# Splitting the first weight load of a decode-attention kernel into 16 and 112 partitions, and moving the small input behind it

## The chip, the cores and the metric

The kernel runs on one core of a Trainium2 chip. The metric is device time in microseconds (us) per execution. The kernel before took 187.73 us at the median of the runs made beside the changed kernel, with a spread of under 0.2 us.

## The reference, cut to what matters

One decode step of attention with grouped heads: 32 sequences, 32 query heads, 8 key/value heads of width 128, a window of the last 512 positions of each cache.

```python
q = (x @ wq)                        # (32, 512) @ (512, 4096)
k, v = k_cache[:, :, -512:], v_cache[:, :, -512:]
p = softmax(q @ k.T * 128 ** -0.5)
out = (p @ v) @ wo                  # (32, 4096) @ (4096, 512)
```

The two windows are 33.5 MB each, `wq` and `wo` 4.2 MB each: 75.5 MB must be read once.

## The kernel before

Everything is written in Bass with explicit semaphores. SP (SyncE) issues nearly all loads on one queue, in a fixed order, and waits only for a buffer to come free. The parts that matter here:

```python
w_sb = sb("w_sb", [P, DKT, HD], BF16)        # 128 partitions x 32 KB
...
nc.scalar.dma_start(x_sb, x.rearrange("b s d -> b (s d)")).then_inc(sem_x, 16)   # 32 KB, ACT's queue
wq_rows = wq.rearrange("(p t) n -> p (t n)", t=DKT)
wq_half = DKT * HD // 2
nc.sync.dma_start(                            # first half of wq: 128 rows of 16 KB
    w_sb[:, 0:2, :].rearrange("p k n -> p (k n)"), wq_rows[:, 0:wq_half]
).then_inc(sem_wq[0], 16)
...
# SP: the second half of wq, then K and V blocks of 2 MB each, then wo
sp.dma_start(w_sb[:, 2:4, :]..., wq_rows[:, wq_half:]).then_inc(sem_wq[1], 16)
for name in DMA_ORDER: ...
...
# TensorE: transpose x, then q = x @ wq in two halves
pe.wait_ge(sem_x, 16)
...
for kt in range(DKT):
    if kt % 2 == 0:
        pe.wait_ge(sem_wq[kt // 2], 16)
    for k in range(2):
        for c in range(4):
            ins = pe.matmul(X_ps[32 * c:32 * c + 32, k, :], lhsT=xT_sb[:, kt, :], rhs=w_sb[:, kt, ...], ...)
```

Each load of this kernel adds 16 to its semaphore, in 16 steps of one that the trace shows one by one; I call these steps its marks. The packet records show sixteen packets of 4 bytes at the end of each load, some 0.4 us before its marks (7.52 to 7.95 us for the first half of `wq`, its marks 7.92 to 8.32), so I read each mark as the end of a sixteenth of the load. Between 4 and 170 us, 15 to 17 packets of 16 KB were under way 99% of the time. "Engine" below means one of the 16 DMA engines that the profile's page counts; the records do not name the engine of a packet or of a mark, so what is said of single engines is read from the order in time.

## Time and profile before

| | before |
|---|---|
| median time, us | 187.73 |
| span of the profiled run, us | 185.9 |
| first packet of the stream / last mark of the last load, us | 1.81 / 182.90 |
| marks of the first half of wq, first to last, us | 7.92 to 8.32 |
| marks of the second half of wq, us | 12.81 to 13.22 |
| mean time of one 16 KB packet in steady flow (packets 33 to 128), us | 0.611 |

The span is measured from the first to the last recorded instruction of the core; the median time is some 1.8 us longer. The profile's page gives busy shares, and its DMA row the share of 40 slices in which the 16 DMA engines were at work. The trace also holds every DMA packet (start, length, bytes) and every semaphore mark. The lines themselves are in the prediction below, which reads them.

### The profile page before, as it was taken

What the parts mean: (1) busy time and instruction counts of PE and PEld (TensorE: products, weight loads), DVE (VectorE), ACT (ScalarE), POOL (GpSimd) and SP (SyncE); (2) the same over time, 40 slices, a digit from 0 to 9 for tenths busy, and PEclk for the clock granted to TensorE, in tenths of its full rate; (3) what the DMA queues carried; (4) which work ended last, traced back from release to release, by engine and by line L of the source; (5) the groups of instructions that cost most, each with busy time, mean ns of one, the idle gap of its engine ahead of it and who ended that gap; (6) DMA issues with size and microseconds to landing.
All of it is one profiled execution on the core that took longest, in us unless ns stands there. A gap on an engine that the chain in (4) does not pass through costs nothing.

```text
span 185.9 us, 3841 instructions
## 1 busy us (share of the span) xinstructions
PE 110.3 (59%) x1604; PEld 90.7 (49%) x1604; DVE 131.8 (71%) x239; ACT 82.4 (44%) x142; POOL 32.1 (17%) x82
## 2 busy tenths in 40 slices
PE   0232004346179925949726992459699975999851
PEld 0100001032069804929326881129669974999741
DVE  0006999689999799985899959999999993010001
ACT  3001000259420199011992039826989999711011
POOL 7100390500700071050420060000030000000000
PEclk9999999999999995796955899657999999699999
DMA  6999999999999999999999999999999999999980
GB/s 208 419 444 423 430 430 419 444 423 426 426 419 430 426 419 430 434 419 434 418 430 430 423 434 412 441 430 416 432 416 430 423 430 426 423 430 404 401 326 25
DMA packets 6160, 75.80 MB, mean 408 GB/s; under 512 B 704, under 2 KB 768, under 8 KB 1792
## 3 DMA queue, kind: packets, MB, share of 16 engines
q1 hardware_dynamic: 6096, 75.53, 96.2%
q8 instruction: 12, 0.20, 0.4%
q10 hardware_dynamic: 48, 0.03, 0.1%
q14 instruction: 4, 0.03, 0.0%
HBM read 75.53 MB, written 0.03 MB: 406 GB/s over the span
## 4 chain that ended last, share of the span: by engine, by line
DMA 58%; DVE 22%; PE 11%; issue 4%; SPq 3%; ACT 0%; DVEq 0%
DMA V_sb<-in_v_cache_dram 31%; DVE KT_sb L426 14%; DMA w_sb<-in_wo_dram 12%; DMA K_sb<-in_k_cache_dram 8%; PE O_ps L353 7%; DMA w_sb<-in_wq_dram 6%; DVE w_sb L448 4%; DVE QA_sb L416 2%; PE S_ps L316 2%; SPq L211 2%; PE X_ps L296 1%; PE PT_ps L335 1%; SPq L200 1%; DVE oT_sb L409 0%; DVE KT_sb L404 0%
## 5 line engine op out<-in xcount | busy, mean ns | idle before, releaser
L426 DVE STREAM_TRANSPOSE KT_sb<-K_sb 128x2048 uint32<-128x2048 uint32 x32 | 72.3, 2287 | 1.2 <-DMA K_sb<-in_k_cache_dram 1.1
L353 PE MATMUL O_ps<-w_sb,V_sb 128*128 128x128 bf16 x640 | 46.1, 241 | 10.5 <-DMA V_sb<-in_v_cache_dram 5.6
L353 PEld LDWEIGHTS O_ps<-w_sb,V_sb 128*128 128x128 bf16 x640 | 44.7, 109 | 13.7 <-issue 7.0
L265 POOL COPY QBD<-QA_sb 32x64 bf16<-32x64 bf16 x64 | 25.6, 540 | 79.6 <-PE S_ps L316 62.0
L515 ACT ACTIVATE w_sb<-PTc,mask 128x512 bf16<-128x512 bf16 x60 | 38.9, 729 | 0.0
L316 PE MATMUL S_ps<-KT_sb,QBD 128*32 128x512 bf16 x256 | 20.9, 479 | 26.3 <-DVE KT_sb L426 19.8
L448 DVE TENSOR_SCALAR w_sb<-PTc,mask 128x512 bf16<-128x512 bf16 x100 | 30.2, 370 | 4.9 <-PE O_ps L353 4.9
L316 PEld LDWEIGHTS S_ps<-KT_sb,QBD 128*32 128x32 bf16 x256 | 7.8, 110 | 35.9 <-issue 32.0
L487 ACT ACTIVATE X_ps<-S_ps,negmax 128x512 f32<-128x512 f32 x8 | 5.3, 659 | 42.2 <-DVE negmax L435 42.2
L335 PE MATMUL PT_ps<-P_bf,pick 128*128 128x128 bf16 x128 | 11.8, 265 | 18.0 <-ACT P_bf L496 14.7
L335 PEld LDWEIGHTS PT_ps<-P_bf,pick 128*128 128x128 bf16 x128 | 10.2, 122 | 20.9 <-ACT P_bf L496 16.3
L525 ACT ACTIVATE oT_sb<-O_ps 128x128 bf16<-128x128 f32 x8 | 6.0, 750 | 26.0 <-PE O_ps L353 26.0
L515 ACT ACTIVATE K_sb<-PTc,mask 128x512 bf16<-128x512 bf16 x24 | 15.3, 717 | 1.6 <-DVE KT_sb L426 1.6
L353 PE MATMUL O_ps<-K_sb,V_sb 128*128 128x128 bf16 x256 | 15.1, 217 | 1.3 <-DMA V_sb<-in_v_cache_dram 1.0
L353 PEld LDWEIGHTS O_ps<-K_sb,V_sb 128*128 128x128 bf16 x256 | 14.5, 96 | 2.1 <-issue 1.3
L448 DVE TENSOR_SCALAR K_sb<-PTc,mask 128x512 bf16<-128x512 bf16 x40 | 12.1, 377 | 0.3 <-ACT PTc L506 0.2
L353 PE MATMUL O_ps<-KT_sb,V_sb 128*128 128x128 bf16 x128 | 9.1, 240 | 2.4 <-DMA V_sb<-in_v_cache_dram 2.4
L353 PEld LDWEIGHTS O_ps<-KT_sb,V_sb 128*128 128x128 bf16 x128 | 8.9, 108 | 2.5 <-issue 2.5
L469 DVE CAST K_sb<-S_ps 128x256 bf16<-128x256 f32 x1 | 0.4, 424 | 12.7 <-PE S_ps L365 12.7
L515 ACT ACTIVATE KT_sb<-PTc,mask 128x512 bf16<-128x512 bf16 x12 | 7.8, 725 | 0.0
L467 DVE CAST K_sb<-X_ps 128x384 bf16<-128x384 f32 x1 | 0.6, 558 | 9.8 <-PE X_ps L365 9.8
L496 ACT ACTIVATE P_bf<-X_ps,recip 128x512 bf16<-128x512 f32 x8 | 5.5, 685 | 4.4 <-DVE recip L441 4.4
(41 smaller groups left out, 49.5 us busy)
## 6 DMA issues: line engine op xcount, KB each, us to landing
K_sb<-in_k_cache_dram SPq DMA_DIRECT2D x16, 2048.0 KB, 15.2
V_sb<-in_v_cache_dram SPq DMA_DIRECT2D x16, 2048.0 KB, 17.0
w_sb<-in_wq_dram SPq DMA_DIRECT2D x2, 2048.0 KB, 9.7
w_sb<-in_wo_dram SPq DMA_DIRECT2D x8, 512.0 KB, 20.3
oT_sb<-in_x_dram ACTq DMA_DIRECT2D x1, 32.0 KB, 4.5
out_dram<-oT_sb SPq DMA_DIRECT2D x1, 32.0 KB, 1.5
```

The lines of the kernel that those rows point to most:

```text
L211: sp.dma_start(wo_sb[:, hg].rearrange("p i n -> p (i n)"), wo[hg * 512:(hg + 1) * 512, :].rearrange("(m i) n -> m (i n)", i=4),).then_inc( ...
L265: pool.tensor_copy(dst[:, i, :, x0:x0 + 4], src).then_inc(pool_qbd, 1)
L316: ins = pe.matmul(S_ps[32 * c:32 * c + 32, q % 2, :], lhsT=QBD[:, q % 2, g, b, e, :], rhs=bass.AP(tensor=KT_sb, offset=s0 * slot + (b * G ...
L335: ins = pe.matmul(PT_ps[:, r, :], lhsT=pick[:, r, KS - s:KS - s + P], rhs=P_bf[:, s, :], start=(s == 0), stop=(s == KS - 1), tile_position ...
L353: ins = pe.matmul(O_ps[:, q % 2, 0:P], lhsT=V_sb[:, m % NV, r, :], rhs=z_of(q)[:, :, x0 + r, :], start=(e == 0 and r == 0), stop=(e == 1 a ...
L416: dve.tensor_copy(QA[32 * a:32 * a + 32, c], QW[32 * c:32 * c + 32, :, :, a::4].rearrange("p h k q -> p h q k"),).then_inc(dve_q, 1)
L426: dve.transpose(KT_w[:, n % NK, b].rearrange("p i r s -> p r i s"), K_w[:, n % NK, :, 32 * b:32 * b + 32],).then_inc(dve_T, 1)
L448: ins = dve.tensor_scalar(z_of(q)[:, k].rearrange("p x r -> p (x r)"), PTc[:, q % RING].rearrange("p x r -> p (x r)"), mask[:, k:k + 1], N ...
L487: act.activation(P_f32, S_ps[:, q % 2, :], ACTF.Exp, bias=negmax[:, q:q + 1], scale=SCALE, accum_out=sums[:, q:q + 1],).then_inc(act_exp, 1)
L496: act.activation(P_bf[:, :, :], P_f32.rearrange("p (x s) -> p s x", s=KS), ACTF.Copy, scale=recip[:, q:q + 1],).then_inc(act_P, 1)
L515: ins = act.activation(z_of(q)[:, k].rearrange("p x r -> p (x r)"), PTc[:, q % RING].rearrange("p x r -> p (x r)"), ACTF.Copy, scale=mask[ ...
L525: act.activation(oT_sb[:, :, 4 * q:4 * q + 4].rearrange("p h a -> p a h"), O_ps[:, q % 2, 0:P].rearrange("p (a h) -> p a h", a=4), ACTF.Co ...
```

## The change

The intent, as I read it: the first load is cut so that its first piece has sixteen rows, as many as there are packets under way at a time, in the hope that all of them start at once; and `x` leaves ACT's queue, where its packets (2.64 to 4.91 us) come between those of the first load.

```diff
-        nc.scalar.dma_start(x_sb, x.rearrange("b s d -> b (s d)")).then_inc(sem_x, 16)
         wq_rows = wq.rearrange("(p t) n -> p (t n)", t=DKT)
         wq_half = DKT * HD // 2
-        nc.sync.dma_start(
-            w_sb[:, 0:2, :].rearrange("p k n -> p (k n)"), wq_rows[:, 0:wq_half]
-        ).then_inc(sem_wq[0], 16)
+        for p0, p1 in ((0, 16), (16, P)):
+            nc.sync.dma_start(
+                w_sb[p0:p1, 0:2, :].rearrange("p k n -> p (k n)"), wq_rows[p0:p1, 0:wq_half]
+            ).then_inc(sem_wq[0], 16)
+        nc.sync.dma_start(x_sb, x.rearrange("b s d -> b (s d)")).then_inc(sem_x, 16)
...
-                    pe.wait_ge(sem_wq[kt // 2], 16)
+                    pe.wait_ge(sem_wq[kt // 2], 32 - 8 * kt)
```

The number of bytes, and the order of all compute instructions on every engine, stay as they were.

## The prediction

Passages that rest on things which no trace or run of this case shows are cut from the prediction, and from the expectations further down; the cuts are marked. One of them takes a term out of the forecast's sum. The sum came to +1.5 us, so 189.2 us, from three terms: -0.2 (an earlier start) and -0.07 (`x`), and the cost of the 16-row load. Of the rivals, the first is that the 16 rows cost no more than their bytes (given a third). Two more are given an eighth and a quarter; the second of these was that the 112 rows cost more than their bytes too. In the list of signs, those before its second cut belong to a slow 16-row load, those after it to one that costs its bytes alone.

> **What bounds the kernel now.** I read the page first (span, busy shares, DMA row, chain), then the landing times of the loads, then fine windows over the two ends of the run, then the packet records of the first microseconds. From the page:
>
> ```profile
> span 185.9 us, 3841 instructions
> PE 110.3 (59%) x1604; PEld 90.7 (49%) x1604; DVE 131.8 (71%) x239; ACT 82.4 (44%) x142; POOL 32.1 (17%) x82
> DMA  6999999999999999999999999999999999999980
> GB/s 208 419 444 423 430 430 419 444 423 426 426 419 430 426 419 430 434 419 434 418 430 430 423 434 412 441 430 416 432 416 430 423 430 426 423 430 404 401 326 25
> ...
> q1 hardware_dynamic: 6096, 75.53, 96.2%
> ...
> DMA 58%; DVE 22%; PE 11%; issue 4%; SPq 3%; ACT 0%; DVEq 0%
> ```
>
> No compute engine is above 71%, while the DMA row is full in every slice except the first and the last two, at some 425 GB/s. 75.53 MB at that rate are 178 us of the 185.9. So the kernel is one stream of loads with a start and a tail. The landing records say the same more sharply: the first of the 16 completion marks of each 2 MB load follows that of the load before by 4.88 to 4.98 us from beginning to end, so the earliest of the 16 DMA engines never runs dry. A compute wait in the middle costs nothing; a microsecond at the head of the stream comes out at the end. Windows of the start (window, length, the five engines, clock, DMA share, GB/s):
>
> ```profile
> 0.00:1.75 1.75, 0.00 (x0) 0.00 (x0) 0.00 (x0) 0.51 (x1) 0.92 (x8) 1.00 0.00 0
> 1.75:4.00 2.25, 0.00 (x0) 0.00 (x0) 0.00 (x0) 0.98 (x2) 2.10 (x3) 1.00 0.91 288
> 4.00:8.00 4.00, 0.28 (x4) 0.21 (x4) 0.29 (x1) 0.00 (x0) 1.43 (x7) 1.00 1.02 436
> ```
>
> Nothing moves before 1.75; the next 2.25 us run at 288 GB/s instead of 436, a loss of 2.25 x (1 - 288/436) = 0.76 us. That is all a better head could recover beyond the start itself. The timeline gives the issues, and the chain the tail:
>
> ```profile
> 0.80 0.41 ACTq L156 DMA_DIRECT2D oT_sb<-in_x_dram  x1
> ...
> 0.80 0.39 SPq L159 DMA_DIRECT2D w_sb<-in_wq_dram  x1
> ...
> 1.24 0.42 SPq L192 DMA_DIRECT2D w_sb<-in_wq_dram  x1
> ```
>
> ```profile
> 159.94 22.96 DMA w_sb<-in_wo_dram
> 182.90 0.04 issue
> 182.94 0.44 PE X_ps L388 x16
> ```
>
> The last wo mark at 182.90 starts a fixed tail of 3.0 us. The 16 marks of that load spread over 3.27 us (179.63 to 182.90) where those of the first load spread over 0.41, so the slowest engine sets the end.
>
> **The head, packet by packet.** The first packets (16 KB rows) start one engine after another from 1.81 to 2.41, one or two later still: a mean start near 2.08. They take 0.78 to 1.42 us, about 1.07, against 0.611 in steady flow. Packets of x, on ACT's queue, come in between from 2.64 on; five of them take 0.18 to 0.36 us instead of 0.045. The final store[...], starts its engines within some 0.12 us (184.91 to about 185.03). [...] The change aims at this.
>
> [...]
>
> **The change part by part.** (1) The first 2 MB load becomes 256 KB for partitions 0 to 15 and 1.75 MB for the rest. Bytes are unchanged; one more issue on SP costs about 0.4 us there, hidden because each 2 MB keeps the queue busy for 4.9 us. The second issue is at about 1.24, and its first rows should be ready near 2.25 (1.24 plus the 1.01 us between issue and first packet, 0.80 to 1.81), while the first row is in flight. Gain: the stagger mean goes from 0.27 to perhaps 0.05, so -0.2 us. (2) x leaves ACT's queue: its five slow packets cost about 1.2 us over 16 engines, -0.07 us each; its 32 KB still pass. x lands behind the first wq half instead of at 5.27. Transpose and evacuation take about 0.6 us and the first half's matmuls 1.9 us, but the second half lands 4.9 us after the first: 2.4 us of slack. The chain through q starts at the second half as before, so this costs nothing. [...] I put the number slightly lower, at 189.0, because the rivals below pull further down than up in weight.
>
> **The rivals.** [...] Then only -0.2 to -0.6 remains, counting that the first packet may also start 0.1 to 0.15 us earlier: the final store's first packet came 0.85 us after its issue began, the first load's 1.01. Time 187.1 to 187.5. For it: the change was evidently meant so, and 0.76 us is there to be had. [...] *It is hidden* fails on the full DMA row: there is no slack for a delayed head to vanish in. *A new wait on x* would need more than the 2.4 us of slack. One disturbance stays: twelve instruction-fetch packets of about 1.05 us fall on single engines in mid-run[...].
>
> **Range and chances.** 187.1[...] to 191.0[...] should hold it 8 times in 10. Two per cent are 3.75 us: a gain like that is impossible when only 1.81 us come before the first packet and 0.76 us are lost after it[...]. Faster 0.01, same 0.91, slower 0.08.
>
> **What would show each step.** [...] a low rate in the window 1.75 to 4, the last mark of the second wq half past 14.3 instead of 13.22, and all later landings shifted alike. [...] sixteen first packets starting within 0.1 us, taking about 1.1 us, and the second wq half landing near 12.8. [...] If x matters, the wait before the second wq half's matmuls ends on something other than the load. The prediction is wrong if the second wq half lands earlier than before, or if the head is delayed and the end is not.

## The result, and the profile after

| | before | after |
|---|---|---|
| median time, us | 187.73 | 191.15 |
| all runs, us | 187.68 to 187.83 | 190.72 to 191.47 |
| ratio | | 1.0178 (1.0161 to 1.0195) |
| span of the profiled run, us | 185.9 | 189.0 |
| last mark of the first half of wq, us | 8.32 | 11.58 |
| last mark of the second half of wq, us | 13.22 | 16.43 |
| last mark of the last load (wo), us | 182.90 | 185.96 |

The changed kernel is 3.42 us slower by the medians: within 2%, and 0.15 us above the stated range.

From the page of the changed kernel (span; DMA busy tenths and GB/s in 40 slices; the chain that ended last, by engine):

```profile
span 189.0 us, 3842 instructions
...
DMA  6999999999999999999999999999999999999980
GB/s 118 319 347 440 423 416 437 433 413 433 437 421 411 437 433 420 426 426 423 430 428 430 420 430 433 430 420 426 428 416 426 433 423 420 433 426 401 407 340 24
...
DMA 55%; DVE 25%; PE 11%; SPq 4%; issue 4%; DVEq 0%
```

The busy row is the same digit for digit, but the first three slices moved 118, 319 and 347 GB/s instead of 208, 419 and 444; from the fourth slice on the two rows are alike to some 5%. So the engines were occupied all the time and moved less. The busy share alone would have hidden it.

Windows of the head of the changed kernel (window, length, busy time of the five engines, clock, DMA share, GB/s). A packet counts, whole, in the window in which it starts, so a share can pass 1:

```profile
1.75:4.00 2.25, 0.00 (x0) 0.00 (x0) 0.00 (x0) 0.54 (x2) 2.10 (x3) 1.00 1.28 233
4.00:8.00 4.00, 0.00 (x0) 0.00 (x0) 0.00 (x0) 0.00 (x0) 1.43 (x7) 1.00 0.88 262
8.00:12.00 4.00, 0.10 (x4) 0.13 (x4) 0.00 (x0) 0.00 (x0) 0.00 (x0) 1.00 1.01 307
```

Before, the first two of these windows had 288 and 436 GB/s, and the third this line:

```profile
8.00:12.00 4.00, 1.90 (x16) 0.54 (x16) 0.00 (x0) 0.00 (x0) 0.00 (x0) 1.00 1.01 434
```

In time at 430 GB/s, 2.25 x (288 - 233) / 430 = 0.29 us are lost in the first window, 4 x (436 - 262) / 430 = 1.62 in the second and 4 x (434 - 307) / 430 = 1.18 in the third: 3.09 us, the whole difference of the spans. Most of it is lost after 4 us, that is, while the 112-row load runs.

The issues in the timeline, and the DMA list (KB each, us from issue to landing), of the changed kernel:

```profile
0.80 0.84 SPq L159 DMA_DIRECT2D w_sb<-in_wq_dram  x2
...
1.70 0.42 SPq L162 DMA_DIRECT2D oT_sb<-in_x_dram  x1
...
2.15 0.42 SPq L193 DMA_DIRECT2D w_sb<-in_wq_dram  x1
```

```profile
w_sb<-in_wq_dram SPq DMA_DIRECT2D x1, 2048.0 KB, 14.3
w_sb<-in_wq_dram SPq DMA_DIRECT2D x1, 1792.0 KB, 10.3
w_sb<-in_wq_dram SPq DMA_DIRECT2D x1, 256.0 KB, 4.2
oT_sb<-in_x_dram SPq DMA_DIRECT2D x1, 32.0 KB, 10.1
```

The issues are done by 2.57 us and were never late. But 256 KB took 4.2 us from issue to landing; before, a load eight times as large landed 7.5 us after its issue. The packet records show the rest: the sixteen rows of the small load start between 1.82 and 2.48 us and take 0.71 to 1.75 us; the next sixteen packets, the first of the 112-row load, take 1.59 us at the mean, and the later ones 0.75 to 1.09 us instead of 0.611.

The tail is unmoved: 185.96 to 189.0 after, 182.90 to 185.9 before, 3.0 us in both.

```profile
164.60 21.36 DMA w_sb<-in_wo_dram
185.96 0.04 issue
186.01 0.44 PE X_ps L389 x16
```

### The profile page after: what moved, and what is told of

The parts are those of the page before. It is cut to its first block, busy times and chain, and to the rows that moved or that the text cites. A ratio compares the mean times of both kernels' runs of the same rounds, so it can differ in the third digit from the quotient of the medians.

```text
span 189.0 us, 3842 instructions
## 1 busy us (share of the span) xinstructions
PE 108.9 (58%) x1604; PEld 89.5 (47%) x1604; DVE 131.7 (70%) x239; ACT 82.3 (44%) x142; POOL 32.0 (17%) x82
## 4 chain that ended last, share of the span: by engine, by line
DMA 55%; DVE 25%; PE 11%; SPq 4%; issue 4%; DVEq 0%
DMA V_sb<-in_v_cache_dram 30%; DVE KT_sb L427 15%; DMA w_sb<-in_wo_dram 11%; DMA w_sb<-in_wq_dram 8%; PE O_ps L354 7%; DMA K_sb<-in_k_cache_dram 6%; DVE w_sb L449 6%; SPq L212 2%; DVE QA_sb L417 2%; PE S_ps L317 2%; PE X_ps L297 1%; DVE maxv L434 1%; SPq L201 1%; SPq L159 0%; DVE oT_sb L410 0%
## 5 line engine op out<-in xcount | busy, mean ns | idle before, releaser
L354 PE MATMUL O_ps<-w_sb,V_sb 128*128 128x128 bf16 x640 | 46.9, 244 | 9.8 <-DVE w_sb L449 5.0
L354 PEld LDWEIGHTS O_ps<-w_sb,V_sb 128*128 128x128 bf16 x640 | 45.5, 111 | 12.5 <-DVE w_sb L449 6.5
L516 ACT ACTIVATE K_sb<-PTc,mask 128x512 bf16<-128x512 bf16 x24 | 15.3, 721 | 1.6 <-DVE KT_sb L427 1.6
L354 PE MATMUL O_ps<-KT_sb,V_sb 128*128 128x128 bf16 x128 | 7.5, 217 | 2.0 <-DMA V_sb<-in_v_cache_dram 2.0
L354 PEld LDWEIGHTS O_ps<-KT_sb,V_sb 128*128 128x128 bf16 x128 | 7.3, 96 | 2.1 <-issue 2.1
L482 ACT ACTIVATE KT_sb<-X_ps 128x512 bf16<-128x512 f32 x1 | 0.6, 597 | 16.1 <-PE X_ps L297 16.1
```

What stands on the lines that cost most here:

```text
L354: ins = pe.matmul(O_ps[:, q % 2, 0:P], lhsT=V_sb[:, m % NV, r, :], rhs=z_of(q)[:, :, x0 + r, :], start=(e == 0 and r == 0), stop=(e == 1 a ...
L516: ins = act.activation(z_of(q)[:, k].rearrange("p x r -> p (x r)"), PTc[:, q % RING].rearrange("p x r -> p (x r)"), ACTF.Copy, scale=mask[ ...
```

## The experiments

Three theories could explain slow packets at the head. The **partition theory**: what a load costs depends on which partitions it writes, and the loads of 16 and 112 partitions cost more than their bytes. A figure that follows a cut without a theory's name is this theory's, unless the text beside it says otherwise. The **issue theory**: more and smaller transfers on one queue, and a late `x`, are what cost. The **memory theory**, a guess to be tested: neighbouring rows of `wq`, read by sixteen packets at once, collide on the HBM side. Differences below are between medians of the same rounds. All twelve kernels gave the right result.

### The second part alone: x behind, no split

```diff
-        nc.scalar.dma_start(x_sb, ...).then_inc(sem_x, 16)
         nc.sync.dma_start(w_sb[:, 0:2, :]..., wq_rows[:, 0:wq_half]).then_inc(sem_wq[0], 16)
+        nc.sync.dma_start(x_sb, ...).then_inc(sem_x, 16)
```

> Kernel before with only the second part of the change: x on the sync queue behind the first wq half, no split. [...] no cost, 187.5 to 187.8 us, and the first packets no longer interrupted by x. Issue theory (more issues on one queue and a late x are what cost): a good part of the 3.4 us, say 188.5 to 190.

Measured: 187.88 us against 187.85, ratio 1.000 (0.9985 to 1.0015). Moving `x` neither costs nor gains. It lands at 8.30 us instead of 5.27. The second half of wq lands at 13.08 instead of 13.22, but nothing of this is left at the end.

### The first part alone: the split, x on ACT's queue

```diff
-        nc.sync.dma_start(x_sb, ...).then_inc(sem_x, 16)      # of the changed kernel
+        nc.scalar.dma_start(x_sb, ...).then_inc(sem_x, 16)    # as before
```

> Changed kernel with x put back on ACT's queue: only the 16/112 split is left. [...] nearly the whole loss, 190.8 to 191.5 us, second wq half landing near 16.4. Issue theory with x as the cause: near 188.

Measured: 191.35 us against 187.85, +3.50 us, ratio 1.0183 (1.0168 to 1.0198). The split is the whole loss.

### The same sizes, cut by columns

```diff
-        for p0, p1 in ((0, 16), (16, P)):
-            ... w_sb[p0:p1, 0:2, :] ..., wq_rows[p0:p1, 0:wq_half]
+        for n0, n1 in ((0, 1024), (1024, wq_half)):
+            ... w_half[:, n0:n1], wq_rows[:, n0:n1]           # w_half: w_sb[:, 0:2] flattened
```

> Changed kernel, but the first load is cut by columns instead of partitions: again 256 KB first and 1.75 MB behind it, same number of issues, same queue, x behind; each load covers all 128 partitions (2 KB and 14 KB rows). [...] the loss is gone, 187.5 to 188.2 us[...]. Issue theory: the loss stays, about 191.

Measured: 187.77 us against 187.85, ratio 0.9996 (0.9979 to 1.0013). The same two sizes, the same issues on the same queue in the same order: no loss. Only the packets are shorter (2 KB and 14 KB). The windows of this kernel, columns as above:

```profile
1.75:4.00 2.25, 0.00 (x0) 0.00 (x0) 0.00 (x0) 0.54 (x2) 2.10 (x3) 1.00 0.98 320
4.00:8.00 4.00, 0.00 (x0) 0.00 (x0) 0.00 (x0) 0.00 (x0) 1.44 (x7) 1.00 1.00 418
```

The rate between 4 and 8 us is 418 GB/s where the changed kernel had 262. The issue theory falls. A small first load shows no gain either, though the interval (-0.39 to +0.24 us) does not rule out the 0.2 us that the prediction hoped for.

### The disputed cost by itself: 16 rows, two sets of partitions

These kernels are the kernel before with one more load behind the second half of wq, in full flow, into a buffer that is not yet in use; its result is not read. TensorE waits for it together with the second half, so that no race arises. Only the target partitions differ:

```diff
+            spare = KT_sb[:, 0].rearrange("p b i r s e -> p (b i r s e)")
+            sp.dma_start(spare[0:16, 0:wq_half], wq_rows[0:16, 0:wq_half]).then_inc(sem_wq[1], 16)
...
-                    pe.wait_ge(sem_wq[kt // 2], 16)
+                    pe.wait_ge(sem_wq[kt // 2], 16 + 8 * kt)
```

with `spare[32:96:4, ...]` in the second kernel.

> Kernel before plus one extra load of 16 rows of 16 KB (256 KB, result unused) behind the second wq half, in full flow, into partitions 0 to 15. [...] Issue theory: only its bytes, 0.61 us, so 188.3 to 188.5. Memory theory (neighbouring rows of wq read by all engines at once collide in HBM): also slow, about 190.

> The same 16 source rows, same packets and same place in the queue, but into partitions 32, 36, ... 92, [...] 0.6 us, so 188.3 to 188.5 us. Memory theory: as slow as into partitions 0 to 15, about 190. Issue theory: 188.3 to 188.5, as for partitions 0 to 15.

The partition theory's figure for the first of the two was a cost well above that of the bytes. Measured: 190.33 against 187.89, +2.44 us, for partitions 0 to 15; 188.49, +0.60 us, for partitions 32, 36, ... 92. Sixteen packets of 16 KB from the same source rows cost four times as much in one set of partitions as in the other. 262,144 bytes in 2.44 us are 107 GB/s. The memory theory falls, since the reads are the same.

One rival is left: the sixteen rows might go four at a time and not sixteen, and 4 x 0.611 us are 2.44 us as well. The packet records rule it out. Then every packet would take 0.611 us. In the low set, the packets that start between 12.3 and 15.3 us take 0.6 to 2.09 us, 34 of them over 0.7, with sixteen under way at once; in the spread one, every packet there takes 0.611. The windows from 13 to 15 us agree: 123 GB/s are 15 packets of 16 KB in 2 us, and a DMA share of 0.77 is 24.6 us of 16 engines' time, 1.64 us for each packet; 442 GB/s at 1.04 come to 0.62. First the low set, then the spread one:

```profile
13.00:15.00 2.00, 0.00 (x0) 0.00 (x0) 0.00 (x0) 0.00 (x0) 0.00 (x0) 1.00 0.77 123
15.00:18.00 3.00, 1.90 (x16) 0.46 (x16) 0.09 (x1) 0.09 (x1) 0.00 (x0) 1.00 0.92 382
```

```profile
13.00:15.00 2.00, 0.86 (x12) 0.33 (x16) 0.00 (x0) 0.00 (x0) 0.00 (x0) 1.00 1.04 442
15.00:18.00 3.00, 1.04 (x12) 0.13 (x4) 1.81 (x4) 0.60 (x1) 0.00 (x0) 1.00 1.01 431
```

The stream falls to 123 GB/s for 2 us in one and runs on at 442 in the other.

### 64 rows, moved by 32 partitions

The same edit with `spare[0:64, ...]` and `spare[32:96, ...]`, both from source rows 0 to 63.

> Extra load of 64 rows of 16 KB (1 MB) into partitions 0 to 63, in full flow. Its bytes alone take 2.44 us. [...] 190.1 to 190.3.

> The same 64 source rows into partitions 32 to 95. [...] 2.44 us, so 190.1 to 190.3 us. [...] and it would take over 5 us, over 192.8. Memory theory: same time as partitions 0 to 63.

In the first of the two, 190.1 to 190.3 us is the time of the bytes alone; the partition theory's figure: a longer time. In the second, 2.44 us is the partition theory's, and "over 5 us" belongs to a variant in which the move of the target would not help. Measured: +5.25 us (193.14 against 187.89) for partitions 0 to 63, +2.47 us (190.36) for 32 to 95. Partitions 0 to 63 first:

```profile
13.00:15.00 2.00, 0.00 (x0) 0.00 (x0) 0.00 (x0) 0.00 (x0) 0.00 (x0) 1.00 1.20 246
15.00:18.00 3.00, 0.00 (x0) 0.00 (x0) 0.00 (x0) 0.00 (x0) 0.00 (x0) 1.00 0.84 186
```

```profile
13.00:15.00 2.00, 0.00 (x0) 0.00 (x0) 0.00 (x0) 0.00 (x0) 0.00 (x0) 1.00 1.01 434
15.00:18.00 3.00, 1.75 (x16) 0.45 (x16) 0.00 (x0) 0.00 (x0) 0.00 (x0) 1.00 1.02 437
```

Moving a 64-row target by 32 partitions halves its cost, down to that of its bytes (64 x 0.611 / 16 = 2.44 us). Why these partitions are the cheaper ones, no trace here shows.

### 112 rows, and 128 as a control

The same edit with `spare[16:128, ...]` and with all of `spare`, from the source rows of the same numbers.

> Extra load of 112 rows of 16 KB into partitions 16 to 127 in full flow; its bytes alone take 4.28 us. [...] more than the 128 rows of the control beside it. If only the 16-row load is to blame for the change's 3.4 us: 192.0 to 192.3.

> Control: extra load of all 128 rows of 16 KB, 2 MB, in full flow. Every theory: 4.9 us, so 192.7 to 192.9 us.

The partition theory's figure for the 112 rows is cut; that they would cost more than the 128 rows is left of it. Measured: 112 rows +6.86 us (194.58 against 187.72), 128 rows +4.88 us (192.60). The smaller load costs 2 us more than the larger one. Its bytes would take 4.88 x 112 / 128 = 4.27 us, so 2.59 us come on top. What causes them is not shown. The 112 rows first:

```profile
13.00:17.00 4.00, 0.00 (x0) 0.00 (x0) 0.00 (x0) 0.00 (x0) 0.00 (x0) 1.00 1.05 283
```

```profile
13.00:17.00 4.00, 0.00 (x0) 0.00 (x0) 0.00 (x0) 0.00 (x0) 0.00 (x0) 1.00 1.03 442
```

The DMA share is as good as the same, 1.05 and 1.03; the rates are 283 and 442 GB/s.

### The small load at the head

The kernel before with an extra load of 16 rows in front of the unsplit first half, into the low and the spread set of partitions:

```diff
+        nc.sync.dma_start(
+            KT_sb[0:16, 0].rearrange("p b i r s e -> p (b i r s e)"), wq_rows[0:16, 0:wq_half]
+        ).then_inc(sem_wq[0], 16)
         nc.sync.dma_start(w_sb[:, 0:2, :]..., wq_rows[:, 0:wq_half]).then_inc(sem_wq[0], 16)
```

with `KT_sb[32:96:4, 0]` in the second kernel. TensorE's wait for the first half is raised to 32, as in the changed kernel.

> Extra load of 16 rows into partitions 0 to 15 as the very first load, in front of the unsplit first wq half (x stays on ACT). [...] 1 to 2.4 us over before; [...] so 188.8 to 190.3 us. [...]

> The same extra first load into the sixteen partitions 32, 36, ... 92. [...] 0.6 us over before less what a small first load gains at the start (predicted 0.2), so 188.2 to 188.5 us; if a small first load gains nothing, 188.5.

Measured: +1.74 us (189.46 against 187.72) for the low set, +0.80 us (188.52) for the spread one. The low partitions cost 0.94 us more than the spread ones at the head, where in full flow the difference is 2.44 - 0.60 = 1.84.

The two traces differ in one thing more, so this pair is not a clean one. In the spread run `x`, issued by ACT at the same moment (0.80 us), went first: it landed 1.7 us after its issue, and the first packet of the stream started at 2.19 us. In the low run it landed after 4.5 us and the stream started at 1.81. The low run first:

```profile
oT_sb<-in_x_dram ACTq DMA_DIRECT2D x1, 32.0 KB, 4.5
oT_sb<-in_x_dram ACTq DMA_DIRECT2D x1, 32.0 KB, 1.7
```

So 0.37 us of the +0.80 may be a later start, and the pair does not tell whether a small first load gains something. Counted against its bytes instead, 0.61 us, the low set costs 1.74 - 0.61 = 1.13 us at the head.

### The partitions, or an odd multiple of sixteen rows?

The 112 rows could also be slow by their number alone: they are seven times sixteen, while the loads that cost no more than their bytes (16 rows spread, 64 rows in 32 to 95, 128 rows) are one, four and eight times sixteen. The odd-count theory, a guess, is that any number of sixteens that is no power of two is slow. Partitions 16 to 63 give three:

```diff
+            sp.dma_start(spare[16:64, 0:wq_half], wq_rows[16:64, 0:wq_half]).then_inc(sem_wq[1], 16)
```

> Extra load of 48 rows of 16 KB into partitions 16 to 63 in full flow; its bytes alone take 1.83 us. [...] or of any load whose rows for each engine are not a power of two (three here, seven there)? [...] Odd-count theory: the factor of the 112 rows, 6.86/4.28 = 1.6, so 2.9 us and 190.6 to 190.9.

Measured: +5.92 us (193.64 against 187.72) for 768 KB, whose bytes alone would take 1.83 us. The odd-count theory, with the factor of the 112 rows, gave 2.9 us and falls in that form. The window shows the stream at a third of its rate (158 GB/s) with the DMA share at 1.04, so all sixteen engines were occupied and slow:

```profile
15.00:18.00 3.00, 0.00 (x0) 0.00 (x0) 0.00 (x0) 0.00 (x0) 0.00 (x0) 1.00 1.04 158
```

No experiment gave a version faster than both kernels; the column split and the moved `x` alone came out level with the kernel before. The 112 and the 48 rows were not tried in other partitions, so the control that settled the 16 and 64 rows is missing for them.

## Why the prediction was right or wrong

**What bounds the kernel: right.** The DMA stream was named as the bound, and a delay of the head was to come out whole at the end. The second half of wq landed 3.21 us later (16.43 - 13.22), the last mark 3.06 us later (185.96 - 182.90), and the span grew by 3.1. The tail kept its 3.0 us. The rival "it is hidden" failed as said.

**Step 1, a stagger gain of 0.2 us: not borne out.** The stagger was taken to grow with the number of rows; these runs do not show that. With 16 rows the first packets still started one after another, from 1.82 to 2.48 us (before, with 128 rows, fifteen from 1.81 to 2.41 and one at 2.68); their mean start went from 2.09 to 1.99 only, and in the run with `x` behind and no split it was 1.97. These packets took longer, too: 1.27 us at the mean instead of 1.06, in the unsplit run 1.26. No gain was seen at the end: the column split changed the time by -0.08 us, though its interval does not rule out -0.2. What does set the stagger stays open.

**Step 2, x: right.** It was to cost nothing and to give at most 0.07 us; the ratio was 1.000.

**Step 3, the 16-row load: it does cost more than its bytes, but the term was too large for the head.** It was close to the measured difference of the two sets of partitions in full flow, 1.84 us. At the head that was 0.94 by the pair of runs and 1.13 by its bytes. That part of it lies beside the start-up, when the first packets are slow anyhow (1.06 us at the mean in the kernel before), is my reading and was not tested. Of the foreseen signs, a low rate from 1.75 to 4 us (233 GB/s instead of 288) and a late second half of wq (16.43 us) appeared; first packets as slow as the term asked for did not: they took 0.71 to 1.75 us, and the next sixteen, already of the 112-row load, took 1.59 us at the mean.

**The step that failed is the sum.** The sum of +1.5 us has no term for the 112-row load. A higher cost of it was put among the rivals (a quarter). Measured in full flow, the 112 rows cost 2.59 us beyond their bytes. With 0.94 us that makes 3.53, against 3.50 for the split alone and 3.42 for the whole change; but the terms come from different places of the stream, and with 1.13 it is 3.72, so some luck is in that agreement.

The packet records of the changed kernel give both terms in place. I take the 16 KB packets in order of start, sixteen at a time (as many as were under way), and compare their mean length with the kernel before. The first sixteen lost 0.21 us each and the next 0.96, as in the run with the low load before an unsplit one (0.19 and 0.90); I count both to the 16 rows. The other six sixteens of the 112-row load lost 1.82 in all, and the eight of the load behind it 0.39. Less the 0.10 us of earlier start, that is 1.07 + 2.21 = 3.28 us, where the second half of wq landed 3.21 us later. So the missing term was the larger one, some 2.2 us, and the cost of the 16 rows at the head was some 1.1 us, not the 1.84 of full flow.

The number was then moved down to 189.0 on account of the rivals with shorter times, so two errors pointed the same way (the oversized term for the 16 rows hid a part of them), and the range ended 0.15 us below the median. What the 112 rows cost is plain in the records: packets of 0.75 to 1.09 us against 0.611, and a first half of wq whose marks spread over 0.94 us instead of 0.41.

**The chances: right in the class**, within 2%, though at 1.0178 by a small margin.

## What to carry to other kernels

In these runs a load that did not cover all 128 partitions could run far below the rate of the stream (16 rows at a quarter, 2.44 us against 0.61 for the bytes; 64 at half, 5.25 against 2.44; 112 at some 60% of it, 6.86 against 4.27), and the choice of partitions decided it, shown for two sizes: the same 16 rows cost 2.44 us or 0.60, and the same 64 rows 5.25 or 2.47. The cause is not shown, so try the partitions that you need. To send a small piece ahead, cut the load by columns so that every piece covers all partitions; that cost nothing here (ratio 0.9996), though it showed no gain either. When a stream of transfers is the bound, read its GB/s and not its busy share (283 against 442 GB/s at shares of 1.05 and 1.03), and when a cost is found for one piece of a cut, work it out for the other piece too.
